# Four query tiles transposed through DRAM and VectorE, and a routing table built from sign steps, in a fused attention and expert kernel

## The chip, the core and the metric

The kernel runs on one core of a Trainium2 chip. A core has a matrix engine (TensorE, PE in the profile; its weight loads are PEld), a vector engine (VectorE, DVE), an activation engine (ScalarE, ACT), a general engine (GpSimd, POOL) and an engine that issues transfers (SyncE, SP). Each works through its own list of instructions in the order in which the program issues them and waits on semaphores for the others. On-chip memory is SBUF (128 partitions); TensorE writes to PSUM, from which VectorE and ScalarE read. DRAM is reached by transfers (DMA), which SP and POOL issue here. The metric is the device time of one execution in microseconds (us).

## The reference

Two branches are added to the input x (2048 tokens of 512 values): linear attention over the normalized input, and a mixture of 8 experts of which each token uses its 2 best.

```python
xn = layernorm(x)
# A: 32 heads of 16
q, k, v = split(xn @ wqkv)
phi = lambda t: where(t > 0, t + 1, exp(t)) + 1e-6
kv = einsum("bhsd,bhse->bhde", phi(k), v);  z = phi(k).sum(tokens)
o = einsum("bhqd,bhde->bhqe", phi(q), kv) / (einsum("bhqd,bhd->bhq", phi(q), z) + 1e-6)
A = o.reshape(B, S, D) @ wo
# B: top 2 of 8 experts, softmax over the two logits
logits = xn @ w_gate;  gates = softmax(top 2 of logits)
B = sum over experts e of gate[e] * (silu(xn @ w1[e]) @ w2[e])
out = x + A + B
```

## The kernel before

The tokens are cut into 16 tiles of 128 (`NT`). Products keep near-full precision by splitting each operand into a high and a low part and adding three products, high by high, high by low, low by high (`PASSES`); a projection of a tile over 512 values is therefore 12 matmuls (4 slices of 128 by 3 passes). The high part is a copy on ScalarE (`split_hi`, line 141), the low part a subtraction on VectorE (`split_lo`, line 144).

The program runs in stages, each handed to the engines in program order (the manual schedule), so the order of the calls in the code is the order on every engine:

1. Load, layer norm and the projection of k for all tiles, and the sums that give the matrix M (kv times wo, kept as high and low parts in `M_v`).
2. The q tiles. This is the stage that the change touches. Tile numbers t run from 0; the code's tiles 6 to 9 are the seventh to the tenth.
3. The experts in 8 rounds, one weight pair after another; tokens are gathered from DRAM, the results are scattered into the output.
4. In the last expert round and behind it, the output projections of the last five q tiles (`ND = 5`, `NO = 11`).

In stage 2 a loop runs over t = 4 to 13. A q tile goes through these calls:

- `q_proj(t)`: 12 matmuls (line 1376), then three activations on ScalarE (lines 1385 to 1387) that leave exp(min(q, 0)).
- `q_phi`, `q_mult` (together `q_feat`): VectorE adds max(q, 0) (line 1393), POOL multiplies by z (line 1397).
- `q_den(t - 1)` and `q_norm(t - 1)`, an iteration later: VectorE sums each head and takes the reciprocal (lines 1410 to 1415), POOL multiplies (line 1416).
- `q_transp(t - 2)`: four transposes on TensorE (line 1422) into PSUM, whose high and low parts go to `pqT`.
- `o_proj(t - 3)`: 12 matmuls with M (line 1437); each group of three reads the high part twice and the low part in its third. `o_out(t - 4)`, an iteration later, adds the result to x on VectorE (line 1478) and stores it (line 1480).

Tiles 11 to 15 take another way: after `q_norm` they are stored to DRAM (`pz_out`), read back late in the last expert round in four pieces that set 32-row blocks side by side (`pz_in`, line 1447), transposed on VectorE in 32 x 32 blocks (`q_turn`, line 1454), and split by `q_hi` and `q_lo`.

Into the same loop other work is woven. The routing's steps (`routing`, a generator; `side` hands out pieces until their costs reach `PERIOD = 2.6`) end in iteration 6 with each token's lane and block. `table(q)` for q = 0 to 3 in iterations 7 to 10 builds two one-hot arrays of 4 tiles each on VectorE, `ohl` over the 128 lanes (line 645) and `mvb` over the 66 blocks, times the token number (lines 647 and 650). `table_mm(q)` multiplies them on TensorE in 8 small matmuls (line 660), an iteration later (the list `late`, run as `due`); the last one runs at the end of iteration 10. `table_end` in iteration 11 (lines 666 to 673) turns the sums into the row numbers `gidx` and `sidx`. From iteration 11 on, `gather1` fetches the first expert's tokens on POOL (line 1047), `x_block` transposes them on TensorE (line 1093), and `plain_w` splits the first weights (ScalarE and VectorE, lines 141 and 144) that `fetch_w` has loaded since iteration 8.

SBUF tiles come from pools: `ta` (11 buffers of 520 words a partition), `um` and `tb` (20 of 1152 words), `sm` (18 of 1024 words), `stage` (3, for weights). A new tile waits until a buffer of its pool is free.

Of the kernel before, what the change touches and what calls it, by code (L numbers as in the profile page):

```python
# [20 lines left out]
P = 128  # L21
# [25 lines left out]
NO = NT - ND  # L47
NE = 12
# [37 lines left out]
def linear_attn_plus_moe(  # L86
# [25 lines left out]
    xs_d = tc.dram_tile((E * RB * P, D), F32, name="xs_d")  # L112
    gate_d = tc.dram_tile((E, BLK, P), F32, name="gate_d")
# [112 lines left out]
    def constants_b():  # L226
# [13 lines left out]
        iota(i_lane, [[1, P]])  # L240
        iota(i_blk, [[1, NB]])
# [202 lines left out]
    lane_f = rt.tile([P, NT, 2], F16, name="lane_f")  # L444
# [11 lines left out]
    def routing():  # L456
# [177 lines left out]
        V.tensor_copy(blk_f, la_i)  # L634
        yield 3.0

    tabp = {}

    def table(q):
        ts = slice(4 * q, 4 * q + 4)  # L640
        ohl = ta(f"ohl{q}", 8 * P, F16).rearrange("p (a b) -> p a b", a=8)
        mvb = ta(f"mvb{q}", 8 * NB, F16).rearrange("p (a b) -> p a b", a=8)
        la = lane_f[:, ts, :].rearrange("p t k -> p (t k)").unsqueeze(2)
        bl = blk_f[:, ts, :].rearrange("p t k -> p (t k)").unsqueeze(2)
        V.tensor_tensor(ohl, i_lane.unsqueeze(1).broadcast_to([P, 8, P]),
                        la.broadcast_to([P, 8, P]), op=ALU.is_equal)
        V.tensor_tensor(mvb, i_blk.unsqueeze(1).broadcast_to([P, 8, NB]),
                        bl.broadcast_to([P, 8, NB]), op=ALU.is_equal)
        m4 = mvb.rearrange("p (t k) b -> p t (k b)", k=2)
        V.tensor_tensor(m4, m4, i_tok[:, ts].unsqueeze(2).broadcast_to([P, 4, 2 * NB]), op=ALU.mult)  # L650
        tabm[q] = (ohl, mvb)

    tabm = {}

# [7 lines left out]

    def table_end():
        tab = wp.tile([P, 2, NB], F32, tag="tab", name="tab", bufs=1)
# [11 lines left out]
    def side_jobs():  # L676
        yield from routing()
        for q in range(4):
            table(q)
            late.append(lambda q=q: table_mm(q))  # L680
            yield 9.0
        table_end()
# [685 lines left out]
    pq, pz, pqT = {}, {}, {}  # L1368
# [43 lines left out]
    def q_norm(t):  # L1412
        den = dens.pop(t)
        V.tensor_scalar(den, den, 1e-6, None, op0=ALU.add)
        V.reciprocal(den, den)
        G.tensor_tensor(heads(pz[t]), heads(pq[t]),
                        den.unsqueeze(2).broadcast_to([P, H, DH]), op=ALU.mult)
# [21 lines left out]

    def pz_out(t):  # L1440
        Q.dma_start(pz_d[(t - NO) * P:(t - NO + 1) * P, :], pz.pop(t))

    def pz_in(t):
        pz[t] = ta(f"pzr{t}")
        rows = pz_d[(t - NO) * P:(t - NO + 1) * P, :].rearrange("(c j) (a f) -> a j c f", j=BLK, f=P)
        for a in range(4):
            Q.dma_start(pz[t][a * BLK:(a + 1) * BLK].rearrange("j (c f) -> j c f", f=P), rows[a])

    def q_turn(t):
        src = pz.pop(t).rearrange("p (c k i) -> p c k i", i=BLK, k=KC)  # L1450
        pz[t] = ta(f"pzt{t}")
# [4 lines left out]
    def q_hi(t):  # L1456
        pqT[t] = tb(f"pqT{t}").rearrange("p (h c) -> p h c", h=2)
        split_hi(pqT[t][:, 0], pz[t])
# [71 lines left out]

    for t in range(OLAG + 1, NT - 2):
        if t < NO + OLAG:
            o_out(t - OLAG - 1)
        due, late[:] = late[:], []
# [6 lines left out]
        q_den(t - 1)  # L1541
        if 8 <= t < 11:
            fetch_w()
        q_proj(t)
        for f in due:
            f()
        if t in (11, 12):
            gather1(0, 2 * t - 22)
        if t == 12:
            x_block(0, 0)  # L1550
# [3 lines left out]
        if t > NO:  # L1554
            pz_out(t - 1)
# [3 lines left out]
        if t < NO + 2:  # L1559
            load_x(t - 2)  # L1560
            q_transp(t - 2)
# [4 lines left out]
        while 3 in tabm:  # L1566
            late.pop(0)()
        if t in (11, 12):
            gather1(0, 2 * t - 21)
# [210 lines left out]
```

## Time and profile before

| | us |
|---|---|
| median of 3 runs (lowest, highest) | 826.55 (826.29, 827.29) |
| profiled execution | 826.48 |
| its span, from the first to the last instruction | 824.8 |
| TensorE busy | 820.3 (99%) |
| VectorE busy | 679.6 (82%) |
| ScalarE busy | 541.2 (66%) |
| POOL busy | 249.7 (30%) |

Rows of the order in time have the start and the duration in us, the engine, the line of the kernel, the instruction, its tiles as output<-input, shapes and a count of merged instructions; in brackets stands how long the engine was idle before it and what ended the wait. Rows of groups have the busy time, the mean in ns of one, and the idle time before them. Matmuls are pipelined: one of 512 columns lasts 0.39 us, but the next starts before it ends, so the distance of their starts is what one costs. A queue name with a q (SPq) marks the issue of a transfer, not its landing.

### The profile page before, as it was taken

How to read it: one execution, taken by the hardware profiler on the slowest of the kernel's cores; microseconds unless marked ns; L12 is line 12 of the kernel's file. 1: busy time of each engine (PE TensorE's matmuls, PEld its weight loads, DVE VectorE, ACT ScalarE, POOL GpSimd, SP SyncE). 2: the span in 40 equal slices, each digit the busy share in tenths (PEclk: the TensorE clock that was granted, in tenths of full speed). 3: DMA queues.
4: the chain of work that ended last, by engine and by line, in shares of the span. 5: the costliest groups of instructions: out<-in, count | busy, mean ns of one | idle time of the engine just before them, and what ended most of it. 6: DMA issues, size and time to landing. Idle time of an engine off the chain costs nothing. (4 is left out here: it accounts for less than half of the span.)

```text
span 824.8 us, 15897 instructions
## 1 busy us (share of the span) xinstructions
PE 820.3 (99%) x5361; PEld 752.1 (91%) x5361; DVE 679.6 (82%) x1470; ACT 541.2 (66%) x1162; POOL 249.7 (30%) x335
## 2 busy tenths in 40 slices
PE   9999999999999999999999999999999999999998
PEld 8999888889999999999999999999999888888886
DVE  7788889999878887878888788789888987887851
ACT  5575364358666768766876777677768766776650
POOL 5543224375310136121803250443127030012002
PEclk9999999999999999999999999999999999999999
DMA  5752136354764565566557464756576573249507
GB/s 168 252 199 87 52 135 202 128 183 166 234 200 135 152 197 108 145 166 184 131 136 187 151 143 136 206 130 161 155 190 130 161 188 113 84 132 232 154 1 178
DMA packets 106874, 127.69 MB, mean 155 GB/s; under 512 B 15198, under 2 KB 69854, under 8 KB 106758
## 3 DMA queue, kind: packets, MB, share of 16 engines
q1 hardware_dynamic: 92902, 106.43, 42.7%
q0 software_dynamic: 12880, 18.66, 11.8%
q10 hardware_dynamic: 1008, 1.57, 0.5%
q8 instruction: 43, 0.70, 0.3%
q14 instruction: 41, 0.34, 0.1%
HBM read 93.95 MB, written 31.09 MB: 152 GB/s over the span
## 5 line engine op out<-in xcount | busy, mean ns | idle before, releaser
L1174 POOL DMA_INDIRECT out_dram<-yo,sidx x22 | 35.1, 1595 | 282.6 <-DVE yo L1169 260.4
L1174 POOL DMA_INDIRECT out_dram<-yu,L x47 | 78.0, 1659 | 85.9 <-ACT yu L1267 59.0
L144 DVE TENSOR_TENSOR h<-hs,h 128x576 fp32r<-128x576 f32 (+7 forms) x112 | 77.7, 694 | 5.7 <-ACT h L141 5.4
L141 ACT ACTIVATE h<-hs 128x576 fp32r<-128x576 f32 (+7 forms) x112 | 72.3, 646 | 3.2
L1324 ACT ACTIVATE hs<-px 128x276 f32<-128x276 f32 (+7 forms) x54 | 21.1, 390 | 58.7 <-PE px L1316 58.6
L1339 ACT ACTIVATE hs<-hs 128x276 f32<-128x276 f32 (+7 forms) x54 | 23.0, 426 | 46.5 <-DVE hs L1338 46.5
L1338 DVE TENSOR_TENSOR hs<-pz,hs 128x276 f32<-128x276 f32 (+7 forms) x54 | 23.3, 431 | 34.6 <-PE pz L1316 34.0
L1343 DVE TENSOR_TENSOR hs<-px,hs 128x276 f32<-128x276 f32 (+7 forms) x54 | 23.3, 432 | 33.7 <-PE px L1316 33.7
L1047 POOL DMA_INDIRECT xg<-xn_d,gidx x37 | 40.8, 1104 | 28.2 <-DMA xq<-xs_d 7.2
L437 PE MATMUL gacc<-pkhl,xnhl 128*128 128x512 f32 x192 | 47.9, 397 | 0.0
L437 PEld LDWEIGHTS gacc<-pkhl,xnhl 128*128 128x128 f32 x192 | 34.8, 188 | 6.8
L1173 POOL MEMSET spacer<- 1x1 f32 x69 | 38.4, 557 | 6.8 <-DVE ws_3l L144 6.8
L1349 DVE TENSOR_TENSOR hs<-py,hs 128x276 f32<-128x276 f32 (+7 forms) x54 | 23.0, 426 | 13.7 <-PE py L1316 13.4
L1344 ACT ACTIVATE hs<-hs 128x276 f32<-128x276 f32 (+7 forms) x54 | 22.8, 422 | 17.0 <-DVE hs L1343 15.8
L411 POOL TENSOR_TENSOR zz<-zz,pk 128x512 f32<-128x512 f32 x14 | 18.2, 1300 | 48.3 <-DVE L L404 48.3
L1385 ACT ACTIVATE e_q<-qp 128x512 f32<-128x512 f32 x16 | 9.6, 598 | 35.4 <-PE qp L1376 31.7
L1198 PE MATMUL y<-w_1h,h 128*128 128x512 f32 (+2 forms) x88 | 32.0, 394 | 0.0
L1198 PE MATMUL y<-w_5h,h 128*128 128x512 f32 (+2 forms) x88 | 32.0, 394 | 0.0
L1198 PE MATMUL y<-w_2h,h 128*128 128x512 f32 (+2 forms) x88 | 32.0, 393 | 0.0
L1198 PE MATMUL y<-w_3h,h 128*128 128x512 f32 (+2 forms) x88 | 32.0, 393 | 0.0
L1198 PE MATMUL y<-w_0h,h 128*128 128x512 f32 (+2 forms) x88 | 32.0, 393 | 0.0
L1198 PE MATMUL y<-w_4h,h 128*128 128x512 f32 (+2 forms) x88 | 31.7, 393 | 0.0
(563 smaller groups left out, 3152.8 us busy)
## 6 DMA issues: line engine op xcount, KB each, us to landing
wst<-in_B_w_dram SPq DMA_DIRECT2D x196, 128.0 KB
wst<-in_B_w_dram SPq DMA_DIRECT2D x37, 512.0 KB
zz<-in_B_w_dram SPq DMA_DIRECT2D x26, 512.0 KB
xs_d<-xg SPq DMA_DIRECT2D x117, 64.0 KB
xq<-xs_d SPq DMA_DIRECT2D x28, 256.0 KB
x<-in_A_x_dram SPq DMA_DIRECT2D x27, 256.0 KB
xn_d<-xn SPq DMA_DIRECT2D x16, 256.0 KB
xnT<-xn SPq DMA_DIRECT2D x11, 256.0 KB
```

What stands on the lines that cost most here:

```text
L141: A.activation(hi, src, AF.Copy)
L144: V.tensor_tensor(lo, src, raw(hi), op=ALU.subtract)
L437: T.matmul(gacc[d], xnhl[:, a, d * P:(d + 1) * P], pkhl[:, b, :], start=(t == 0 and i == 0), stop=(t == NT - 1 and i == 2))
L1047: G.indirect_dma_start(out=raw(t), out_offset=None, in_=xn_d, in_offset=IOA(ap=gidx[:, b:b + 1], axis=0))
L1173: G.memset(spacer, 0.0)
L1174: st = G.indirect_dma_start(out=rows, out_offset=IOA(ap=idx, axis=0), in_=src, in_offset=None, compute_op=ALU.add).ins
L1198: T.matmul(ya[r, d][:m], h[a][:, d * P:d * P + m], w[b][:, n % 2, :], start=(first and i == 0), stop=(last and i == 2))
L1338: V.tensor_tensor(c12, pz_, c12, op=ALU.add)
L1339: A.activation(c12, c12, AF.Silu)
L1343: V.tensor_tensor(c22, px, c22, op=ALU.add)
L1344: A.activation(c22, c22, AF.Silu)
L1349: V.tensor_tensor(c11, pz_, c11, op=ALU.add)
```

## The change

- Tiles 6 to 9 (`TURNED`) no longer pass through the four transposes on TensorE. `q_norm` writes them in an order of columns that suits the 32 x 32 blocks; in the same iteration they are stored to DRAM (`pz_out`) and read back in four pieces (`pz_in`); an iteration later VectorE turns them (`q_turn`) and ScalarE takes the high part (`q_hi`); at the start of the iteration after that VectorE takes the low part (`q_lo`), behind `o_out`. `o_proj` keeps its place, three iterations behind the projection.
- The lane array is no longer a one-hot from VectorE. ScalarE writes eight rows of sign(lane of the token - i - 0.5) for each table group (`table_lanes`), four behind the exponentials of `q_proj`, four later in the iteration, in iterations 6 to 9. The table's sums are then differences short of a step: after the last table group they are split (`table_split`, start of iteration 11) and multiplied by a two-diagonal matrix (`table_diff`, two matmuls behind `q_proj(11)`), and `table_end` follows, ahead of `q_den(10)`. Five instructions on POOL build the matrix (`table_steps`, iteration 8).
- `fetch_w` of iterations 8 to 10 is issued behind the read-back instead of ahead of the projection. `x_block(0, 0)` moves from in front of the attention's transposes to behind `o_proj(9)` in iteration 12.
- The lane arrays, the read-back and the step matrix use the `um` pool; `pqT` of the turned tiles stays in the `sm` pool.

```diff
@@ -45,6 +45,7 @@
 PASSES = ((0, 0), (0, 1), (1, 0))
 ND = 5
 NO = NT - ND
+TURNED = range(6, NO - 1)
 NE = 12
 NP = NF // 2
 NPLAIN = 2
@@ -110,6 +111,7 @@
     M_d = tc.dram_tile((2, 2, P, SW), F32, name="M_d")
     pz_d = tc.dram_tile((ND * P, D), F32, name="pz_d")
     xs_d = tc.dram_tile((E * RB * P, D), F32, name="xs_d")
+    pq_d = tc.dram_tile((len(TURNED) * P, D), F32, name="pq_d")
     gate_d = tc.dram_tile((E, BLK, P), F32, name="gate_d")
     sx_d = tc.dram_tile((P, BLK), F32, name="sx_d")
 
@@ -238,6 +240,7 @@
         G.affine_select(out=bmask, in_=bmask, pattern=[[DH, 8], [0, DH]],
                         compare_op=ALU.is_ge, fill=0.0, base=DH - 1, channel_multiplier=-1)
         iota(i_lane, [[1, P]])
+        G.tensor_scalar(i_lane, i_lane, 0.5, None, op0=ALU.add)
         iota(i_blk, [[1, NB]])
         iota(i_ov, [[1, NOV]])
         iota(i_e8, [[0, NT], [1, E]], base=-E)
@@ -441,7 +444,7 @@
 
 
     rt = cst
-    lane_f = rt.tile([P, NT, 2], F16, name="lane_f")
+    lane_f = rt.tile([P, NT, 2], F32, name="lane_f")
     blk_f = rt.tile([P, NT, 2], F16, name="blk_f")
     ohr = rt.tile([P, E, E], F32, name="ohr")
     gate = rt.tile([P, OV0], F32, name="gate")
@@ -632,25 +635,43 @@
         V.tensor_copy(lane_f, la_i)
         V.tensor_scalar(la_i, sl_i, 7, None, op0=ALU.arith_shift_right)
         V.tensor_copy(blk_f, la_i)
+        lanes.append(0)
         yield 3.0
 
     tabp = {}
+
+    lanes = []
+
+    def table_lanes(h):
+        if not lanes or lanes[0] == 4:
+            return
+        q = lanes[0]
+        if h == 0:
+            tabm[q] = raw(um(f"ohl{q}"))[:, :4 * P].bitcast(F16).rearrange("p (a b) -> p a b", a=8)
+        la = lane_f[:, 4 * q:4 * q + 4, :].rearrange("p t k -> p (t k)")
+        for i in range(4 * h, 4 * h + 4):
+            A.activation(tabm[q][:, i, :], i_lane, AF.Sign, bias=la[:, i:i + 1], scale=-1.0)
+        lanes[0] += h
 
     def table(q):
         ts = slice(4 * q, 4 * q + 4)
-        ohl = ta(f"ohl{q}", 8 * P, F16).rearrange("p (a b) -> p a b", a=8)
         mvb = ta(f"mvb{q}", 8 * NB, F16).rearrange("p (a b) -> p a b", a=8)
-        la = lane_f[:, ts, :].rearrange("p t k -> p (t k)").unsqueeze(2)
         bl = blk_f[:, ts, :].rearrange("p t k -> p (t k)").unsqueeze(2)
-        V.tensor_tensor(ohl, i_lane.unsqueeze(1).broadcast_to([P, 8, P]),
-                        la.broadcast_to([P, 8, P]), op=ALU.is_equal)
         V.tensor_tensor(mvb, i_blk.unsqueeze(1).broadcast_to([P, 8, NB]),
                         bl.broadcast_to([P, 8, NB]), op=ALU.is_equal)
         m4 = mvb.rearrange("p (t k) b -> p t (k b)", k=2)
         V.tensor_tensor(m4, m4, i_tok[:, ts].unsqueeze(2).broadcast_to([P, 4, 2 * NB]), op=ALU.mult)
-        tabm[q] = (ohl, mvb)
+        tabm[q] = (tabm[q], mvb)
 
     tabm = {}
+
+    def table_steps():
+        step, tabp[2] = ta("step", P), um("step_r")[:, :P]
+        G.memset(step, 0.0)
+        for base, v in ((0, -0.5), (-1, 0.5), (P - 1, -0.5)):
+            G.affine_select(out=step, in_=step, pattern=[[1, P]], compare_op=ALU.not_equal,
+                            fill=v, base=base, channel_multiplier=-1)
+        G.tensor_copy(tabp[2], step)
 
     def table_mm(q):
         if q == 0:
@@ -660,8 +681,18 @@
             T.matmul(tabp[0], ohl[:, i, :], mvb[:, i, :],
                      start=(q == 0 and i == 0), stop=(q == 3 and i == 7))
 
+    def table_split():
+        tab = wp.tile([P, 2, NB], F32, tag="tab", name="tab", bufs=1)
+        hl = um("tabhl")
+        tabp[1] = tab, hl[:, :NB], hl[:, NB:2 * NB]
+        split(*tabp[1][1:], tabp[0])
+
+    def table_diff():
+        for i in range(2):
+            T.matmul(tabp[0], tabp[2], tabp[1][1 + i], start=(i == 0), stop=(i == 1))
+
     def table_end():
-        tab = wp.tile([P, 2, NB], F32, tag="tab", name="tab", bufs=1)
+        tab = tabp[1][0]
         t1, em = tab[:, 0, :], tab[:, 1, :]
         V.tensor_copy(t1, tabp[0])
         V.tensor_scalar(gidx, t1, -1.0, 0.0, op0=ALU.add, op1=ALU.max)
@@ -677,9 +708,10 @@
         yield from routing()
         for q in range(4):
             table(q)
+            if q == 1:
+                table_steps()
             late.append(lambda q=q: table_mm(q))
             yield 9.0
-        table_end()
 
     marks = []
     side = side_jobs()
@@ -1365,7 +1397,7 @@
         Q.dma_start(out[S + i * P:S + (i + n) * P, :].rearrange("(a p) d -> p a d", p=P),
                     zt.unsqueeze(1).broadcast_to([P, n, D]))
 
-    pq, pz, pqT = {}, {}, {}
+    pq, pz, pzt, pqT = {}, {}, {}, {}
 
     eq = {}
 
@@ -1413,8 +1445,11 @@
         den = dens.pop(t)
         V.tensor_scalar(den, den, 1e-6, None, op0=ALU.add)
         V.reciprocal(den, den)
-        G.tensor_tensor(heads(pz[t]), heads(pq[t]),
-                        den.unsqueeze(2).broadcast_to([P, H, DH]), op=ALU.mult)
+        out, src, den = heads(pz[t]), heads(pq[t]), den.unsqueeze(2).broadcast_to([P, H, DH])
+        if t in TURNED:
+            out = pz[t].rearrange("p (a k h d) -> p k a h d", a=4, k=KC, d=DH)
+            src, den = (ap.rearrange("p (k a h) d -> p k a h d", a=4, k=KC) for ap in (src, den))
+        G.tensor_tensor(out, src, den, op=ALU.mult)
 
     def q_transp(t):
         p = psm("tr", f"pqp{t}")
@@ -1437,24 +1472,32 @@
                     T.matmul(op, pqT[t][:, a, kc * P:(kc + 1) * P], M_v[kc // 2][b][:, kc % 2, cols],
                              start=(kc == 0 and i == 0), stop=(kc == KC - 1 and i == 2))
 
+    def rows_d(t):
+        return pq_d[(t - TURNED[0]) * P:(t - TURNED[0] + 1) * P, :] if t in TURNED else \
+            pz_d[(t - NO) * P:(t - NO + 1) * P, :]
+
     def pz_out(t):
-        Q.dma_start(pz_d[(t - NO) * P:(t - NO + 1) * P, :], pz.pop(t))
+        Q.dma_start(rows_d(t), pz.pop(t))
 
     def pz_in(t):
-        pz[t] = ta(f"pzr{t}")
-        rows = pz_d[(t - NO) * P:(t - NO + 1) * P, :].rearrange("(c j) (a f) -> a j c f", j=BLK, f=P)
+        if t in TURNED:
+            both = raw(tb(f"pzr{t}"))
+            pz[t], pzt[t] = both[:, :D], both[:, D:]
+        else:
+            pz[t] = ta(f"pzr{t}")
+        rows = rows_d(t).rearrange("(c j) (a f) -> a j c f", j=BLK, f=P)
         for a in range(4):
             Q.dma_start(pz[t][a * BLK:(a + 1) * BLK].rearrange("j (c f) -> j c f", f=P), rows[a])
 
     def q_turn(t):
         src = pz.pop(t).rearrange("p (c k i) -> p c k i", i=BLK, k=KC)
-        pz[t] = ta(f"pzt{t}")
+        pz[t] = pzt.pop(t) if t in TURNED else ta(f"pzt{t}")
         dst = pz[t].rearrange("p (k c j) -> p c k j", k=KC, j=BLK)
         for q in range(2):
             V.transpose(dst[:, :, 2 * q:2 * q + 2, :], src[:, :, 2 * q:2 * q + 2, :])
 
     def q_hi(t):
-        pqT[t] = tb(f"pqT{t}").rearrange("p (h c) -> p h c", h=2)
+        pqT[t] = (sm if t in TURNED else tb)(f"pqT{t}").rearrange("p (h c) -> p h c", h=2)
         split_hi(pqT[t][:, 0], pz[t])
 
     def q_lo(t):
@@ -1528,9 +1571,16 @@
     q_transp(1)
     q_feat(3)
 
+    done = []
     for t in range(OLAG + 1, NT - 2):
+        diff = done == [table_mm]
+        if diff:
+            table_split()
+            done.append(table_split)
         if t < NO + OLAG:
             o_out(t - OLAG - 1)
+        if t - 3 in TURNED:
+            q_lo(t - 3)
         due, late[:] = late[:], []
         spent = 0.0
         while spent < PERIOD:
@@ -1538,33 +1588,48 @@
             if c is None:
                 break
             spent += c
-        q_den(t - 1)
-        if 8 <= t < 11:
-            fetch_w()
+        if not diff:
+            q_den(t - 1)
         q_proj(t)
+        table_lanes(0)
         for f in due:
             f()
+        if diff:
+            table_diff()
+            table_end()
+            q_den(t - 1)
         if t in (11, 12):
             gather1(0, 2 * t - 22)
-        if t == 12:
-            x_block(0, 0)
         if t == 13:
             gather1(0, 4)
         q_norm(t - 1)
-        if t > NO:
+        if t > NO or t - 1 in TURNED:
             pz_out(t - 1)
         q_feat(t)
         if t == 4:
             Q.dma_start(out[NO * P:S, :], x[NO * P:S, :])
         if t < NO + 2:
             load_x(t - 2)
-            q_transp(t - 2)
+            if t - 1 in TURNED:
+                pz_in(t - 1)
+            if t - 2 in TURNED:
+                q_turn(t - 2)
+                q_hi(t - 2)
+            else:
+                q_transp(t - 2)
+        table_lanes(1)
+        if 8 <= t < 11:
+            fetch_w()
         if t >= 11:
             plain_w()
         if t - OLAG < NO - 1:
             o_proj(t - OLAG)
-        while 3 in tabm:
+        while 3 in tabm and type(tabm[3]) is tuple:
             late.pop(0)()
+            if 3 not in tabm:
+                done.append(table_mm)
+        if t == 12:
+            x_block(0, 0)
         if t in (11, 12):
             gather1(0, 2 * t - 21)
 
```

## The prediction

> **What bounds the kernel now.** I read the page first, then the busy time by stretch, then the order of the instructions of each engine in the stage that the change touches.
>
> ```profile
> span 824.8 us, 15897 instructions
> ...
> PE 820.3 (99%) x5361; PEld 752.1 (91%) x5361; DVE 679.6 (82%) x1470; ACT 541.2 (66%) x1162; POOL 249.7 (30%) x335
> ```
>
> TensorE works 820.3 of 824.8 us, so the time falls only by work taken from TensorE, and rises by every wait put on it. The profiled execution took 826.48 us (1.68 around its span), 0.07 under the median of 826.55; the sum is made against 826.48. A change under 0.2% (1.65 us) can't be told from none here.
>
> ```profile
> 146.00:152.00 6.00, 6.00 (x30) 4.96 (x29) 5.90 (x10) 2.44 (x4) 2.21 (x3) 1.00 0.26 87
> ...
> 170.00:176.00 6.00, 6.00 (x30) 4.93 (x29) 5.65 (x14) 3.39 (x5) 4.87 (x5) 1.00 0.37 74
> ```
>
> By stretch (columns PE, PEld, DVE, ACT, POOL, clock, DMA share, GB/s): in the loop of the q tiles VectorE is as full as TensorE (5.90 of 6.00), ScalarE has 3.5 us to spare, the DMA engines three quarters. TensorE never waits, at full clock. The stage is balanced: each tile passes through all engines once, and whatever is late on VectorE comes to TensorE one or two tiles later.
>
> **1. What TensorE loses and gains.**
>
> ```profile
> 147.02 0.60 PE L1422 MATMUL pqp<-ident_r,pz 128*128 128x128 f32 x4
> ...
> 147.93 0.63 PE L1437 MATMUL op<-M0h,pqT 128*128 128x512 f32 x2
> ...
> 150.23 0.39 PE L1376 MATMUL qp<-wq0h,xnT 128*128 128x512 f32 x1
> ...
> 152.96 0.43 PE L660 MATMUL tabp<-mvb,ohl 128*128 128x66 f16 x8
> ...
> 154.16 0.62 PE L1437 MATMUL op<-M0h,pqT 128*128 128x512 f32 x2
> ...
> 159.83 0.48 PE L1437 MATMUL op<-M0h,pqT 128*128 128x512 f32 x1
> ...
> 168.86 0.43 PE L660 MATMUL tabp<-mvb,ohl 128*128 128x66 f16 x8
> ...
> 169.68 0.63 PE L1376 MATMUL qp<-wq0h,xnT 128*128 128x512 f32 x2
> ...
> 171.98 0.60 PE L1422 MATMUL pqp<-ident_r,pz 128*128 128x128 f32 x4
> ```
>
> A projection's 12 matmuls run from 150.23 to 152.96: 0.2275 each. From a transpose group (147.02) to the third matmul behind it (147.93) is 0.91; without the group it would be 2 x 0.2275, so a group costs 0.46. Behind a table group it is 1.20 with transposes (152.96 to 154.16) and 0.82 without (168.86 to 169.68): 0.38. Four groups go: those of tiles 6, 7, 8 (iterations 8 to 10, behind a table group) and 9 (iteration 11): 3 x 0.38 + 0.46 = 1.6. The two matmuls of table_diff come in: between a quarter of a table group (0.07) and a whole transpose group (0.46); I take half of the latter, 0.2. Net -1.4: 825.1, if nothing waits.
>
> **2. The new path of a q tile.** It was: q_norm (POOL), transposes (PE), hi (ACT), lo (DVE). It becomes: q_norm, pz_out (SP), landing, four pz_in (SP), landing, q_turn (DVE), hi, lo; q_turn two iterations behind the projection, lo three behind.
>
> ```profile
> L1454 DVE STREAM_TRANSPOSE pzt<-pzr x10: 401/419/440, 756.2 to 790.7; 128x256 f32<-128x256 f32 x10
> L141 ACT ACTIVATE pqT<-pzt x5: 615/624/639, 772.2 to 795.7; 128x512 fp32r<-128x512 f32 x5
> L144 DVE TENSOR_TENSOR pqT<-pzt,pqT x5: 682/686/692, 773.0 to 796.6; 128x512 fp32r<-128x512 f32 x5
> ```
> ```profile
> 0.83 0.86 SPq L155 DMA_DIRECT2D x<-in_A_x_dram  x2
> ```
> ```profile
> 3.49 0.69 DVE L273 BATCH_NORM_STATS2 bs<-x 128x6 f32<-128x512 f32 x1 [1.80 <-DMA x<-in_A_x_dram]
> ```
> ```profile
> 228.40 0.43 SPq L1237 DMA_DIRECT2D sx_d<-s_at  x1
> 234.81 1.75 SPq L1241 DMA_DIRECT2D s_in<-sx_d  x4
> ```
> ```profile
> 740.45 1.89 SPq L1447 DMA_DIRECT2D pzr<-pz_d  x4
> ```
>
> The last tiles already go this way: a turn is 2 x 0.42 = 0.84, hi 0.62, lo 0.69. The round trip is not in this stage. The one 256 KB transfer that something waits for at once, at the start, lands 2.66 after its issue (0.83 to 3.49); the four pz_in take 1.89 to issue. Lower end: 2.66 out, and back 2.66 from the first of the four issues: 5.3. Upper end: a store of the later stage, issued at 228.40 amid weight loads, whose reader could issue only at 234.81, 6.4; then 1.89 and 2.2 (2.66 less an issue of 0.43): 10.5. I take 2.66 + 1.89 + 1.9 = 6.5, nearest to the row at the start, as the DMA engines are a quarter to a half busy here; the weight loads behind pz_in are out of the way by the next pz_out.
>
> **3. Does it come in time?** Order of the engines from the code, durations from these rows, 0.1 a hand-over (estimate).
>
> ```profile
> 146.68 0.68 DVE L1478 TENSOR_TENSOR x<-op,x 128x512 f32<-128x512 f32 x1
> 147.28 1.88 DVE L645 TENSOR_TENSOR ohl<-i_lane,lane_f 128x1024 f16<-128x1024 f16 x1
> 149.08 0.70 DVE L647 TENSOR_TENSOR mvb<-i_blk,blk_f 128x528 f16<-128x528 f16 x1
> ...
> 150.44 0.68 DVE L1410 TENSOR_REDUCE den<-pz 128x32 f32<-128x512 f32 x1
> ...
> 151.64 0.63 DVE L1393 SCALAR_TENSOR_TENSOR pq<-qp,e_q 128x512 f32<-128x512 f32 x1
> ```
> ```profile
> 151.86 1.06 POOL L1416 TENSOR_TENSOR pz<-pq,den 128x512 f32<-128x512 f32 x1 [3.79 <-DVE den L1415]
> ```
>
> VectorE in iteration 7: o_out 0.60, lanes 1.80, mvb 1.36, then q_den(6); POOL's q_norm starts 1.42 behind q_den's start. The four lanes groups go (7.2 us of VectorE).
> - Tile 6: q_den at 150.44 - 1.80 = 148.64, q_norm 150.06 to 151.1, pz_out 151.2, + 6.5 = 157.7, turn to 158.65, hi to 159.4, lo to 160.2. o_proj(6) would start at 159.83 - 2 x 0.38 = 159.07, its third matmul (the first to read lo) 0.46 later. It waits 0.4 for hi and 0.3 for lo: **0.7**.
> - Tile 8 and table_diff: behind the turn of 6 VectorE still has lo(6) (160.2), mvb 1.36, then 1.42 to q_norm(8): 162.95, pz_out 164.1, + 6.5 = 170.6, turn(8) to 171.55. Behind it in VectorE's queue stands table_split, and on ScalarE hi(8) in front of its first half: 172.3, 172.6, then the low half: 172.9. table_diff needs it; TensorE is there at 171.98 - 3 x 0.38 + 0.7 = 171.5. It waits **1.4**.
> - o_proj(8): lo(8) is behind table_split and o_out(7): 172.9 + 0.6 + 0.7 = 174.2; its third matmul would be at 173.0 + 0.2 + 0.46 = 173.65. It waits **0.6**.
>
> ```profile
> 171.63 0.22 DVE L666 COPY tab<-tabp 128x66 f32<-128x66 f32 x1
> ...
> 172.88 0.68 DVE L1410 TENSOR_REDUCE den<-pz 128x32 f32<-128x512 f32 x1
> ...
> 175.67 2.43 DVE L144 TENSOR_TENSOR w_0l<-wst,w_0h 128x1024 fp32r<-128x1024 f32 x1
> ...
> 182.16 1.48 DVE L144 TENSOR_TENSOR w_1l<-wst,w_1h 128x1024 fp32r<-128x1024 f32 x1 [0.26 <-ACT w_1h L141]
> ```
> ```profile
> 174.58 1.05 ACT L141 ACTIVATE w_0h<-wst 128x1024 fp32r<-128x1024 f32 x1
> ```
>
> - o_proj(9), the largest: lo(9) stood ahead of the first weight split in iteration 11 and now stands behind it, in iteration 12. From 174.2: table_end 1.25 (171.63 to 172.88), q_den and q_norm 1.20, q_phi 0.55, turn(9) 0.84, hi(9) 0.72, the weights' high half 1.05 (ScalarE, behind hi(9)), their low half 1.6, o_out(8) 0.6, lo(9) 0.8: 182.8. TensorE: o_proj(8) from 173.2, + 0.6 + 24 x 0.2275 + 0.46 (transposes of tile 10) = 179.7, third matmul 180.2. It waits **2.6**, however fast the round trip is.
>
> The weights' low half took 2.43 beside POOL's q_mult and 1.48 in the iteration after. I take 1.48, as it now starts after q_mult(11) has ended; with 2.43 the sum is 1 us more. On this the Trainium skill, SBUF — State Buffer, section "Who interferes with whom", says that a VectorE instruction with two SBUF inputs contends with a GpSimd instruction that reads SBUF; by that rule lo(6), lo(8) and lo(9), which now read both inputs from SBUF, could be held by POOL too, and the sum would be up to 833 (three times the 0.95 between the rows). The two rows agree with it.
>
> Sum: -1.4 + 0.7 + 1.4 + 0.6 + 2.6 = +3.9: **830.3** (826.48 + 3.85 unrounded). Nothing behind this stage gives it back, since TensorE is full to the end.
>
> **4. What costs nothing.** Each at zero for the cover named.
>
> ```profile
> L1267 ACT ACTIVATE yu<-yu,gu 128x128 f32<-128x128 f32 x47 | 15.3, 389 | 1.3 <-DVE yu L1274 1.3
> ...
> L141 ACT ACT_TABLE_LOAD x1 | 1.3, 1283 | 0.8 <-PEq L1769 0.8
> L1296 ACT ACT_TABLE_LOAD x1 | 1.3, 1283 | 0.0
> ```
> ```profile
> masks.py:199 POOL TENSOR_SCALAR_AFFINE_SELECT idt<-idt 128x128 f32<-128x128 f32 x1 | 0.3, 292 | 0.1
> ```
>
> The Sign steps: like yu's (15.3 / 47 = 0.33), eight are 2.6 a tile; ScalarE goes from 2.44 to 5.0 of 5.7 in iterations 6 to 9. The second half stands behind hi, which waits for the turn, so the exponentials behind it can start 1 to 2 late; they have an iteration of slack. table_steps: five instructions of at most 0.3 on POOL, inside its wait of 3.79. On SP, pz_in waits for pz_out's landing with fetch_w and the next o_out store behind it: the weights are wanted from 174.58 on and are asked for from 160 on. q_norm's permuted write I keep at 1.06; were it twice that, each round trip would be 1 longer. x_block(0,0) moves back by a projection: no work more or less.
>
> **Rivals.**
> - *All in time (not slower)*: round trips of 5.3 and the work between table_diff and lo(9) 2.6 shorter than the rows say: 825.1. For it: VectorE loses 7.2 us of lanes. Against it: the order of iteration 12. It decides where lo(9) is ready at 180.2 minus the waits before. 0.20.
> - *The gathers take it back*: TensorE in time, but the first expert's rows not.
>
> ```profile
> 184.80 0.95 POOL L1047 DMA_INDIRECT xg<-xn_d,gidx  x1 [0.30 <-issue]
> ```
> ```profile
> DMA to landing us min/median/max: 5.2/5.2/5.2
> ```
> ```profile
> 190.34 0.80 PE L1093 MATMUL xep<-ident_r,xg 128*128 128x128 f32 x8
> ```
>
> The last gather lands at 190.0 and is read by the second half of the group at 190.34: 0.65 of slack. table_end now comes behind q_proj(11), so TensorE may gain 1.4 and the gathers only some 0.5: it waits about 0.3 to 1.2 and the time is 825.4 to 826.3. 0.10.
> - *Slow round trips*: 8.5 or more, as in the stage with weight loads. Each us counts twice (tiles 6 and 8): over 834.3, and 838.3 at 10.5. 0.12.
> - *Sign reloads the function table*: two loads of 1.28 in each of iterations 6 to 9 make ScalarE 5.0 + 2.6 = 7.6 of 5.7: 4 x 1.9 = 7.6, with the waits for lo(8) and lo(9) 826.48 - 1.4 + 7.6 + 3.2 = 836. The program has two loads in all, so Relu, Exp, Identity and Copy share one. The Trainium skill, ScalarE: Activation LUTs, section "Table sets: the hidden batching unit", has cheap functions in every set and doesn't name Sign among them. 0.03.
>
> **Numbers.** Forecast, a round trip of 5.3 to 8.5: 0.55, its own range 828.2 (the first two waits nearly gone, -1.4 + 0.1 + 0.5 + 2.6) to 834.3. Slower by over 0.2%: 0.55 + 0.12 + 0.03 = 0.70. The first rival's 825.1 is inside 0.2%; I give 0.07 of its 0.20 to faster and 0.13 to same, with the gathers 0.23. The range 825.0 to 834.5 leaves out the slow round trips, the table loads and the low edge of the first rival.
>
> **What would show it.** No transposes of q tiles between 153 and 172; TensorE idle before o_proj(6), table_diff, o_proj(8) and most before o_proj(9), each ended by VectorE's lo or split; VectorE idle before q_turn, ended by the read-back's DMA; SP from pz_out to the last pz_in about 4.5. Wrong if lo(9) runs before TensorE reaches o_proj(9), or if pz_out's landing takes under 1.5.

## The result, and the profile after

| | before | changed |
|---|---|---|
| median of the runs, us | 826.99 (6 runs, 826.29 to 827.33) | 837.43 (6 runs, 834.31 to 838.49) |
| profiled execution, us | 826.48 | 835.63 |
| span, mean granted clock | 824.8, 1.000 | 833.9, 0.998 |

The changed kernel is slower by 1.2% (ratio 1.012, interval 1.0102 to 1.0138). The direction was forecast, the size was not: 830.3 stands against 837.43, and the range ended at 834.5. The runs of the changed kernel lie 4 us apart, with mean clocks of 0.993 to 0.998; those before lie 1 us apart.

First the weight loads of TensorE (PEld) in order of time, only the rows with a wait; in brackets the idle time ahead of the instruction and what ended it.

```profile
159.28 0.30 PEld L1472 LDWEIGHTS op<-M0h,pqT 128*128 128x128 f32 x2 [0.20 <-DVE pqT L146]
...
165.54 0.19 PEld L1472 LDWEIGHTS op<-M0h,pqT 128*128 128x128 f32 x1 [0.83 <-ACT pqT L143]
...
166.27 0.30 PEld L1472 LDWEIGHTS op<-M0h,pqT 128*128 128x128 f32 x2 [0.43 <-DVE pqT L146]
...
174.41 0.30 PEld L692 LDWEIGHTS tabp<-tabhl,step_r 128*128 128x128 f32 x2 [2.87 <-issue]
...
175.55 0.30 PEld L1472 LDWEIGHTS op<-M0h,pqT 128*128 128x128 f32 x2 [0.61 <-DVE pqT L146]
...
182.59 0.19 PEld L1472 LDWEIGHTS op<-M0h,pqT 128*128 128x128 f32 x1 [1.54 <-ACT pqT L143]
...
186.00 0.30 PEld L1472 LDWEIGHTS op<-M0h,pqT 128*128 128x128 f32 x2 [3.11 <-DVE pqT L146]
```

In order these are `o_proj(6)`, twice `o_proj(7)`, `table_diff` ("issue", because the wait is for a split that VectorE ends at 174.3), `o_proj(8)`, twice `o_proj(9)`: 9.6 us together.

What is late lies on SP. Its queue of DMA issues (start, us, what):

```profile
151.59 0.33 SPq L1480 DMA_DIRECT2D pq_d<-pz  x1
...
153.66 1.76 SPq L1490 DMA_DIRECT2D pzr<-pq_d  x4
155.52 0.38 SPq L1523 DMA_DIRECT2D out_dram<-x  x1
156.60 0.34 SPq L1480 DMA_DIRECT2D pq_d<-pz  x1
...
160.57 1.75 SPq L1490 DMA_DIRECT2D pzr<-pq_d  x4
163.41 0.43 SPq L965 DMA_DIRECT2D wst<-in_B_w_dram  x1
163.94 0.45 SPq L1523 DMA_DIRECT2D out_dram<-x  x1
164.44 0.42 SPq L1480 DMA_DIRECT2D pq_d<-pz  x1
...
169.13 1.75 SPq L1490 DMA_DIRECT2D pzr<-pq_d  x4
171.09 0.41 SPq L965 DMA_DIRECT2D wst<-in_B_w_dram  x1
...
172.10 0.42 SPq L1480 DMA_DIRECT2D pq_d<-pz  x1
...
176.60 1.75 SPq L1490 DMA_DIRECT2D pzr<-pq_d  x4
```

And VectorE's turns, with the order behind the last one:

```profile
157.07 0.77 DVE L1497 STREAM_TRANSPOSE pzr<-pzr 128x256 f32<-128x256 f32 x2 [1.10 <-DMA pzr<-pq_d]
...
164.06 0.77 DVE L1497 STREAM_TRANSPOSE pzr<-pzr 128x256 f32<-128x256 f32 x2 [1.72 <-DMA pzr<-pq_d]
...
172.49 0.77 DVE L1497 STREAM_TRANSPOSE pzr<-pzr 128x256 f32<-128x256 f32 x2 [3.17 <-DMA pzr<-pq_d]
...
181.10 0.77 DVE L1497 STREAM_TRANSPOSE pzr<-pzr 128x256 f32<-128x256 f32 x2 [2.75 <-DMA pzr<-pq_d]
183.52 1.23 DVE L146 TENSOR_TENSOR w_0l<-wst,w_0h 128x1024 fp32r<-128x1024 f32 x1 [1.65 <-ACT w_0h L143]
184.66 0.68 DVE L1521 TENSOR_TENSOR x<-op,x 128x512 f32<-128x512 f32 x1
185.27 0.68 DVE L146 TENSOR_TENSOR pqT<-pzr,pqT 128x512 fp32r<-128x512 f32 x1
```

From `pz_out` to the turn (the round trip), tiles 6 to 9 take 5.5, 7.5, 8.05 and 9.0. The way back (first `pz_in` to turn) is 3.4, 3.5, 3.4, 4.5; the landing of `pz_out` (to the first `pz_in`) is 2.1, 4.0, 4.7, 4.5. Ahead of the `pz_out` of tiles 8 and 9 stands a weight load of 512 KB, issued 1.0 earlier. Why the way back of tile 9 is longer than the others isn't shown.

The `pz_out` of tiles 8 and 9 are also issued late. POOL's `q_norm` of these tiles:

```profile
161.94 1.06 POOL L1452 TENSOR_TENSOR pz<-pq,den 128x512 f32<-128x512 f32 x1 [4.11 <-DVE den L1447]
...
168.92 1.06 POOL L1452 TENSOR_TENSOR pz<-pq,den 128x512 f32<-128x512 f32 x1 [4.67 <-DVE den L1447]
```

They end at 163.00 and 169.98. SP is then still at the transfers that stand ahead (the weight load and the store, for tile 9 also the read-back of tile 8), and issues `pz_out` 1.4 and 2.1 later. From the end of `q_norm` to the turn it is 9.5 and 11.1.

Last, the busy time by stretch behind the wait of 3.11; the third number from the end is the granted clock.

```profile
186.00:188.00 2.00, 2.00 (x7) 1.63 (x8) 1.93 (x5) 0.82 (x1) 0.70 (x1) 0.77 0.68 169
188.00:190.00 2.00, 2.00 (x9) 1.51 (x8) 2.00 (x3) 0.00 (x0) 2.00 (x2) 0.50 0.95 354
190.00:192.00 2.00, 2.00 (x10) 1.67 (x10) 1.97 (x4) 0.66 (x2) 1.57 (x2) 0.87 0.89 251
```

TensorE gets half its clock for some 3.4 us: 2 x (0.23 + 0.50 + 0.13) = 1.7 us lost. With the waits of the weight loads the whole is 826.48 - 1.4 (as forecast) + 9.6 + 1.7 = 836.4. The matmuls (PE) end a little after the weight loads begin to wait, and are idle for 7.3 at the same places; with that figure it is 834.1. The measured 835.63 lies between the two.

### The profile page after: what moved, and what is told of

Read it like the earlier page. It is cut to its first block, busy times and chain, and to the rows that moved or that the text cites. A ratio compares the mean times of both kernels' runs of the same rounds, so it can differ in the third digit from the quotient of the medians.

```text
span 833.9 us, 15951 instructions
## 1 busy us (share of the span) xinstructions
PE 821.9 (99%) x5347; PEld 751.4 (90%) x5347; DVE 676.5 (81%) x1475; ACT 551.3 (66%) x1195; POOL 252.5 (30%) x341
## 5 line engine op out<-in xcount | busy, mean ns | idle before, releaser
L1079 POOL DMA_INDIRECT xg<-xn_d,gidx x37 | 39.1, 1056 | 32.0 <-DMA xs_d<-xg 7.3
L1230 PE MATMUL y<-w_6h,h 128*128 128x512 f32 (+2 forms) x88 | 31.6, 394 | 0.0
```

Of the source, the lines that this page charges most:

```text
L1079: G.indirect_dma_start(out=raw(t), out_offset=None, in_=xn_d, in_offset=IOA(ap=gidx[:, b:b + 1], axis=0))
L1230: T.matmul(ya[r, d][:m], h[a][:, d * P:d * P + m], w[b][:, n % 2, :], start=(first and i == 0), stop=(last and i == 2))
```

## The experiments

### The weight loads away from the round trips

```diff
+        if 4 <= t < 7:
+            fetch_w()
         q_proj(t)
...
-        if 8 <= t < 11:
-            fetch_w()
```

> The three first weight loads go out in iterations 4 to 6, ahead of every round trip; all else as changed. In the changed kernel the round trips of tiles 6, 7, 8, 9 (issue of pz_out to start of q_turn) took 5.5, 7.5, 8.1, 9.0. Theory A (what stands just ahead of pz_out in SP's queue makes its landing late, the 256 KB store of o_out most): tile 7 had a store ahead and no weights, so tiles 8 and 9 fall to about 7.5 each; table_diff waits some 0.6 less, o_proj(9) 0.6 to 1 less at its first matmul; about 836 against 837.4. Theory B (the weight loads are the cause): tiles 8 and 9 fall to 5.5 as tile 6; table_diff's wait of 2.9 falls to 0.3 to 0.8 and o_proj(9)'s first wait of 1.5 goes: 833 to 834. If the trips don't change at all, neither holds.

831.03 (ratio to before 1.0043, 1.0029 to 1.0057): 6.4 us of the 10.4 are gone, more than either theory said (between the two profiled executions it is 4.6, 835.63 to 831.07). `q_norm(8)` and SP's queue around tile 8, with a 256 KB store ahead and no weights:

```profile
162.89 1.06 POOL L1452 TENSOR_TENSOR pz<-pq,den 128x512 f32<-128x512 f32 x1 [4.11 <-DMA pzr<-pq_d]
```
```profile
163.12 0.38 SPq L1523 DMA_DIRECT2D out_dram<-x  x1
163.98 0.34 SPq L1480 DMA_DIRECT2D pq_d<-pz  x1
...
166.04 1.74 SPq L1490 DMA_DIRECT2D pzr<-pq_d  x4
```

`pz_out` goes out 0.03 behind the end of `q_norm`. The landing is 2.06 instead of 4.69, the trips of tiles 8 and 9 are at most 5.9 and 5.8. Theory B holds for the trips; the time fell below its 833. The waits of `table_diff`, `o_proj(8)` and the first of `o_proj(9)` are gone. Of TensorE's waits this one is left beside tile 7's 0.51 and 0.43 and tile 6's 0.18:

```profile
181.36 0.30 PEld L1472 LDWEIGHTS op<-M0h,pqT 128*128 128x128 f32 x2 [2.60 <-DVE pqT L146]
```

That is the third matmul of `o_proj(9)`, and the clock falls behind it too (0.72, 0.50, 0.93 from 182 to 188: again 1.7).

### The same loads on another queue

In `fetch_w` the three first loads are issued with `A.dma_start` instead of `Q.dma_start`, in the same iterations.

> The three first weight loads stay at their places in iterations 8 to 10 but are issued on ScalarE's DMA queue instead of SP's; all else as changed. Theory A (a weight load delays the round trip because pz_out stands behind it in the same queue): the landings of pz_out of tiles 8 and 9 fall from 4.7 and 4.5 to 2.1 to 3, and most of what the early loads brought (6.4) comes: 831 to 833. Rival B (the 512 KB take the DMA engines' time, whatever the queue): the landings stay at 4 or more and the time at 835.5 to 837.5.

830.75 (1.0051, 1.0038 to 1.0064). The landings of tiles 8 and 9 fall to 2.7 and 2.1, as theory A says, and their `pz_out` again goes out 0.03 behind `q_norm`. But the run doesn't settle queue against engines: on ScalarE the loads no longer wait behind `pz_in`, and go out 4 to 5.5 us earlier (159.5, 166.2, 173.0; on SP 163.4, 171.1, 178.5). The one at 166.2 now runs beside tile 8's read-back, and that takes 5.7 instead of 3.4; the one at 173.0 runs beside tile 9's, which takes 4.95:

```profile
166.19 0.41 ACTq L961 DMA_DIRECT2D wst<-in_B_w_dram  x1
```
```profile
172.09 0.77 DVE L1516 STREAM_TRANSPOSE pzr<-pzr 128x256 f32<-128x256 f32 x2 [1.61 <-DMA pzr<-pq_d]
...
178.19 0.77 DVE L1516 STREAM_TRANSPOSE pzr<-pzr 128x256 f32<-128x256 f32 x2 [0.19 <-DMA pzr<-pq_d]
```

So the trip itself stays long (8.4 and 7.0): what runs beside a load is slow on the other queue too. Counted from the end of `q_norm`, tiles 8 and 9 reach the turn after 8.4 and 7.1, against 9.5 and 11.1 with the loads on SP and 5.9 and 5.9 with the loads early.

### lo(9) ahead of the weight split

```diff
-        if t - 3 in TURNED:
+        if t - 3 in TURNED and t < 12:
             q_lo(t - 3)
...
+        if t == 11:
+            q_lo(9)
         if t >= 11:
             plain_w()
```

> q_lo(9) stands right behind q_hi(9) in iteration 11, ahead of the first weight split. Theory (the order of VectorE's queue holds o_proj(9), as the prediction says): the wait of 3.1 before its third matmul falls to 0.6 to 0.9 (hi and then lo, 0.63 and 0.68), the one before its first (1.5, the round trip) stays; 2.3 less, and 1 to 2 more if the lower clock that follows goes with it: 833.5 to 835 against 837.4. Rival (the weights' low half is then late and holds the first expert's work): the 2.3 comes back as a wait of TensorE after 190, time within 1 of 837.4.

834.24, 3.2 less, as expected (1.0085, 1.0072 to 1.0099). The wait of 3.11 is 0.43:

```profile
184.21 0.30 PEld L1472 LDWEIGHTS op<-M0h,pqT 128*128 128x128 f32 x2 [0.43 <-DVE pqT L146]
```

Between the profiled executions it is only 1.5 less (835.63 to 834.11): the half clock now follows the wait of `table_diff` (2.97; 0.80, 0.50, 0.85 from 174 to 180), and the first expert's transposes wait 1.12, part of what the rival feared.

### The table's split ahead of q_turn(8)

`table_split()`, `q_turn(8)` and `q_hi(8)` are called in this order behind `table_mm(3)`, at the end of iteration 10.

> table_split stands ahead of q_turn(8) and hi(8) on VectorE and ScalarE (both sit idle there, 169 to 172.5). Theory A (the round trip of tile 8 is the cause, the order only shows it): table_diff no longer waits, but o_proj(8) then waits for hi(8) and lo(8) at nearly the same time, its first matmul at about 174.0 instead of 174.6, its third at 174.7 instead of 175.55; 0.8 less: about 836.6. Rival B (the order is the cause, as the prediction's second wait has it): the whole 2.9 goes: about 834.5 or less.

836.08 (1.0108, 1.0093 to 1.0124). That is nearer to theory A, but 1.4 less than the changed kernel isn't clear of its spread of 4 us. The profile shows where the wait went: `table_diff` waits no more, and `o_proj(8)` takes the wait over:

```profile
174.13 0.19 PEld L1472 LDWEIGHTS op<-M0h,pqT 128*128 128x128 f32 x1 [1.98 <-ACT pqT L143]
```

The order only showed the late trip. Behind `o_proj(9)`, with waits of 1.74 and 3.11, the clock was one half for 6.8 us here (0.53, 0.50, 0.50, 0.76 from 184 to 192).

### TensorE kept busy in its waits

```diff
+    def fill(t, n):
+        pre[t] = psm("acc", f"op{t}_0", D)
+        for _ in range(n):
+            T.matmul(pre[t], M_v[0][0][:, 0, :P], M_v[0][0][:, 0, :], start=True, stop=True)
...
         if diff:
+            fill(8, 13)
             table_diff()
...
+            if t == 12:
+                fill(9, 21)
             o_proj(t - OLAG)
```

> Twelve to thirteen idle matmuls of 128x512 (12 to 13 x 0.2275 = 2.9) are put ahead of table_diff and 21 (4.8) ahead of o_proj(9); they write a PSUM tile that the real group then starts afresh. TensorE works through its waits, which stay as they are. Theory A (the idle TensorE brings the lower granted clock, 0.77, 0.50 and 0.87 in the windows from 186 to 192): the clock stays at 1.00 there, the profiled execution loses 1.7 (835.6 to about 834), the median more (its runs have a mean clock of 0.993 to 0.998), and the runs lie within 1 us of each other. Rival B (the lower clock has another cause, such as the DMA load or the weight splits): the windows from 186 to 192 stay under 0.9 and the time stays at 836 to 838.

The clock does what theory A says: 0.999, 0.999, 1.000, 1.000 in four runs (0.993 to 0.998 without the filling), and behind `o_proj(9)`:

```profile
188.00:190.00 2.00, 2.00 (x10) 1.62 (x10) 1.93 (x6) 0.59 (x1) 0.95 (x1) 1.00 0.86 241
```

The time is 836.19 (834.47 to 836.62), only 1.2 less, which isn't clear of the changed kernel's spread, and its own spread isn't under 1. In the profiled run tile 9's trip took 10.4, and `o_proj(9)` waited another 1.25 behind the filling. That the idle TensorE brings the lower clock is shown; what it costs the median isn't measured by this run.

### Store and load behind the read-back

In the iterations of the trips, SP's order becomes pz_out, pz_in, store of `o_out`, `load_x`.

> In the iterations of the round trips the store of an older tile (256 KB) and the load of x (256 KB) stand behind pz_in in SP's queue instead of ahead of it and beside it; the weight loads stay where the change put them. Theory B (only the weight loads make the trips of tiles 8 and 9 late): these stay at 7.5 to 9, the waits of table_diff (2.9) and o_proj(9) stay, and the time is 836 to 837.5; tile 7's trip (7.5, no weights near it) may fall. Rival A (any 256 KB ahead of or beside pz_out does it): all trips come to 5.5 to 6, the time to 831 to 833, as with the weights moved away (831.03).

838.29 (1.0137, 1.0122 to 1.0152): no gain, so theory B again, but 0.8 worse than it allowed. VectorE's `o_out` then waits 1.2 and 1.4 for the later x, and lo stands behind it. Tile 7's `pz_out` now has the store and the load of the tile before right ahead and lands in 4.6. Why tile 7's landing is late with no weights near (3.6 to 5.0 wherever its `pz_out` comes 5 us behind tile 6's) stays open; it isn't the store alone, since tile 8 had one 0.86 ahead and landed in 2.06. In the run of the turned tiles alone, further down, tile 7's `pz_out` comes 6.1 behind tile 6's, when tile 6's read-back has ended, and lands in 2.04.

### All of these together

> Weight loads in iterations 4 to 6, store and load behind pz_in, table_split ahead of q_turn(8), q_lo(9) ahead of the first weight split. If the waits found so far are all that the change costs, TensorE has none left but some 0.4 where lo follows hi, the clock stays at 1.00, and the four transpose groups stay saved: 826.9 - 1.4 + 0.2 to 0.8, so 825.5 to 826.3, faster than before by 0.1%. Rival: something else of the change costs time (gathers, Sign steps, POOL against VectorE), and it stays over 827.

830.52 (1.0052, 1.0039 to 1.0066). The theory failed: `o_out` waited 1.9 and 1.1 for x in the same way, and `o_proj` 1.9 and 1.4 for lo; the first expert's transposes waited 1.45, which the rival had named with the gathers. Moving store and load was the mistake; it is left out below.

### The table part alone

`TURNED` is empty; everything else as changed.

> The table's part alone: no tile is turned (q tiles 7 to 10 are transposed by TensorE as before), the lanes are Sign steps on ScalarE, table_split and table_diff stay, the weight loads stay behind q_transp. Theory (all of the loss hangs on the round trips): table_diff adds 0.2 and waits at most some 0.5 for its split: 827 to 827.7. Rival (the table part has a cost of its own: the Sign steps on ScalarE, the longer mvb beside POOL, the later table_end): 828.5 or more.

826.81 against 826.87 (1.0002, 0.9993 to 1.0011), and TensorE waits nowhere in this stage, but for the 0.26 at each table group that the kernel before has too. Sign steps, split and difference cost nothing that can be measured: the loss comes with the turned tiles.

### The turned tiles alone

The table as before, on top of the next experiment's two edits.

> The turned tiles alone: the table is built as in the kernel before (one-hot lanes on VectorE, no Sign steps, no table_diff), with the weight loads in iterations 4 to 6 and q_lo(9) ahead of the first weight split. To be read beside the run with the same two edits and the new table (828.06). Theory (VectorE was full, 5.9 of 6.0, and the turn needs the room that the lanes leave): 1.88 - 0.08 more of VectorE in each of four iterations, the turns come 2 to 4 late, TensorE waits, 832 or more. Rival (VectorE's waits for the read-back leave room enough): within 1 of 828.

830.59 (1.0060, 1.0043 to 1.0078), 2.5 more than the same with the new table. The turns of tiles 7 and 8 start without a wait for their read-back (165.56 and 172.26), so VectorE is what is late there. The time lies between the two expectations: the room that the lanes leave on VectorE is needed, but less than I had said.

### Weights early and lo(9) early

> Weight loads in iterations 4 to 6 and q_lo(9) ahead of the first weight split, nothing else. With the weights away (831.03) TensorE still waited 0.2, 0.5, 0.4 at tiles 6 and 7 and 2.6 before the third matmul of o_proj(9), and ran at clocks of 0.72, 0.50 and 0.93 behind that (loss of 1.7). Theory (that wait is VectorE's order, the clock follows from the wait): both go: 831.0 - 2.6 - 1.7 + up to 0.4: 826.7 to 827.2, no difference from before. Rival (the clock falls for another reason): 828 to 829.

828.06 (1.0019, 1.0010 to 1.0028). The wait of 2.60 is gone and the clock is 1.00 in the profiled run, as the theory has it, yet about 1 us is missing: the time is the rival's, its reason is not. TensorE has a new wait, before the first expert's transposes:

```profile
190.95 0.40 PEld L1125 LDWEIGHTS xep<-ident_r,xg 128*128 128x128 f32 x4 [1.33 <-ACT xr L1128]
```

ScalarE is late there, because an exponential found its buffer held by `q_norm` on POOL:

```profile
188.12 0.60 ACT L1417 ACTIVATE e_q<-qp 128x512 f32<-128x512 f32 x1 [1.14 <-POOL pz L1452]
```

POOL had waited 1.1 for denominators behind the weight split, then took 2.27 for a `q_mult` (1.29 before), and its `q_norm(12)` stands behind two gathers:

```profile
181.30 1.06 POOL L1452 TENSOR_TENSOR pz<-pq,den 128x512 f32<-128x512 f32 x1 [1.12 <-DVE den L1447]
182.32 2.27 POOL L1429 TENSOR_TENSOR pz<-pq,zz 128x512 f32<-128x512 f32 x1
184.75 0.99 POOL L1079 DMA_INDIRECT xg<-xn_d,gidx  x1 [0.15 <-POOL pz L1429]
186.04 0.95 POOL L1079 DMA_INDIRECT xg<-xn_d,gidx  x1 [0.30 <-issue]
187.01 1.07 POOL L1452 TENSOR_TENSOR pz<-pq,den 128x512 f32<-128x512 f32 x1
```

### Three steps to a version without waits

Tile 7 transposed again, and the denominators of tile 11 ahead of the weight split:

```diff
-TURNED = range(6, NO - 1)
+TURNED = (6, 8, 9)
...
             q_lo(9)
+            q_den(t)
+            den_inv(t)
```

> A version meant to beat both: weight loads in iterations 4 to 6; tiles 6, 8 and 9 turned, tile 7 transposed by TensorE as before (its trip starts while tile 6's read-back still runs, and it alone still made TensorE wait, 0.6 and 0.43); q_lo(9) and the denominators of tile 11 ahead of the first weight split, so that POOL's q_norm(11) need not wait 1.1 for them. Theory (the wait of 1.3 and 0.3 of the first expert's transposes in the run with the weights away and q_lo(9) moved comes from POOL, whose q_norm held the exponentials): with that wait gone, 826.9 - 3 groups (0.38 + 0.38 + 0.46) + 0.2 for table_diff + 0.2 to 0.5 of waits = 825.9 to 826.3, 0.1% faster. Rival (POOL is full there whatever VectorE does, and takes back what TensorE gains): 826.7 to 827.2.

829.99 (1.0037, 1.0024 to 1.0050); profiled 828.56. All waits of `o_proj` are gone, but the expert's transposes wait 1.20 and 1.73: the last gather is issued at 184.86, as in the kernel before (184.80), whatever TensorE gained. POOL takes the gain back, as the rival says, and the time is over the rival's 827.2 too; the three runs above the profiled one had mean clocks of 0.997 and 0.998. Next the table is ended earlier:

```diff
+            q_proj(t, True, 0)
+            table_diff()
+            table_end()
+            q_lo(t - 3)
+            gather1(0, 0)
+            gather1(0, 1)
```

> As the version meant to beat both (weights in iterations 4 to 6, tile 7 transposed by TensorE, q_lo(9) and the denominators of tile 11 ahead of the first weight split; 829.99, its profiled execution 828.56 with waits of 1.20 and 1.73 before the first expert's transposes), but the table is ended earlier: table_split stands ahead of q_turn(8), table_diff in the middle of q_proj(11), table_end right behind it, and the first two gathers ahead of q_norm(10). POOL sat idle for 3.2 before the first gather, at 172.95. Theory (the gathers and POOL's chain behind them hold TensorE there): the first gather starts at 171 to 171.5, the last some 1.4 earlier, q_norm(12) too; the waits fall from 2.9 to 0 to 1.0 and the time to 826.0 to 827, with the clock at 1.00. Rival (the last gather's landing is late for the DMA engines' load, not for POOL): the second wait stays at 1 or more and the time over 827.5.

827.07 (1.0004, 0.9995 to 1.0013), just over what was expected; the first gather starts at 171.27 as the theory said, the last still at 185.12, which it did not. Of the waits 0.60 and 0.67 are left; POOL stood idle for 1.87 ahead of `q_norm(11)`. So the fourth gather goes into that gap:

> As the version with the table ended early (827.07; its profiled execution had waits of 0.60 and 0.67 before the first expert's transposes, and POOL idle for 1.87 before q_norm(11)), but the fourth gather stands ahead of q_norm(11) on POOL, in that idle time, and q_den(11) ahead of q_lo(9). Theory (what is left of the saving goes into POOL's chain, gathers and q_norm(12)): the last gather starts at about 183 instead of 185.1, q_norm(12) ends 1 to 2 earlier, both waits go, and the time is 825.6 to 826.2, 0.1% under before. Rival (the gathers' landing, not their start, or ScalarE's own order holds the transposes): a wait of 0.6 or more stays there, and the time stays within 0.5 of 827.

826.17 against 826.67 (ratio 0.9993, 0.9984 to 1.0003).

```profile
177.54 0.95 POOL L1079 DMA_INDIRECT xg<-xn_d,gidx  x1 [0.30 <-issue]
178.51 1.63 POOL L1457 TENSOR_TENSOR pz<-pq,den 128x512 f32<-128x512 f32 x1
...
183.82 0.99 POOL L1079 DMA_INDIRECT xg<-xn_d,gidx  x1 [1.90 <-PE qp L1410]
185.02 1.06 POOL L1457 TENSOR_TENSOR pz<-pq,den 128x512 f32<-128x512 f32 x1 [0.21 <-DVE den L1447]
```

The waits of TensorE (PEld) from 150 to 195, summed by line, are in this version

```profile
PEld L681 <- issue: 1.0, 4, 0.3
PEld op L1477 <- DVE pqT L146: 0.2, 1, 0.2
```

and the first row is there before as well (0.8 and 0.3, at `table_mm`). The theory on POOL's chain holds: the last gather starts 1.3 earlier, and both waits are gone. With three of the four tiles turned the change can be had without its losses, and is then even with the kernel before or 0.1% faster; the interval takes in 1.

## Why the prediction was wrong

| TensorE waits for | forecast | measured | with the weights early |
|---|---|---|---|
| `o_proj(6)` | 0.7 | 0.20 | 0.18 |
| `o_proj(7)` | none | 0.83 + 0.43 | 0.51 + 0.43 |
| `table_diff` | 1.4 | 2.87 | none |
| `o_proj(8)` | 0.6 | 0.61 | none |
| `o_proj(9)` | 2.6 | 1.54 + 3.11 | 2.60 |
| sum | 5.3 | 9.6 | 3.7 |

- **The step that failed** is the size of the round trip. I took 6.5 for every tile and wrote that "the weight loads behind pz_in are out of the way by the next pz_out". They are not: `pz_in` holds SP until `pz_out` has landed, and the load goes out behind it. The next tile's `pz_out` is then issued 1.4 to 2.1 behind `q_norm` (0.1 taken) and 1.0 behind the load, and its landing takes 2.6 longer (4.69 against 2.06). Undisturbed the trip is 5.5 to 5.9, under my 6.5; behind a load it is 8 to 9. The bounds of 5.3 and 10.5 held all four tiles. That the loads are the cause is shown by the run that moves them. Whether they act by their place in the queue or by sharing the DMA engines stays open. The Trainium skill, DMA: Bandwidth & Descriptors, section "Queues, rings and completion order", says that each DMA engine takes the descriptors of one ring in order. The landing behind the load agrees with it; that the read-back beside a load of the other queue was slow too (5.7) shows that order isn't all.
- **Luck**: I had `pz_out(8)` at 164.1, and it went out at 164.44. But `q_norm(8)` had ended at 163.00, 1.0 earlier than in my sum, and the queue took that away.
- I had followed SP's queue for what waits behind `pz_in`, and asked only whether the weights would be late. The question left out was what they stand in front of.
- **Tile 7** was not worked out at all. Its trip was 7.5 with no weights near, and cost 1.3.
- **"Slow round trips"**, at 0.12, was the rival that came nearest; its "over 834.3" was right. Its 8.5 or more held for tile 9 alone. That "each us counts twice (tiles 6 and 8)" was wrong: tile 6 came in time, tiles 7, 8 and 9 did not.
- **o_proj(9)**: the cause, lo(9) behind the weight split, was right: lo moved ahead takes the wait away. The 2.60 with the weights early is my 2.6 by luck. TensorE came 1.4 earlier than in my sum, and so did lo; from the turn to lo it took 4.1, not 4.8 (the low half of the weights 1.22, with 1.48 taken). And the turn still waited 0.75 for the read-back there, so "however fast the round trip is" isn't shown.
- **The clock** had no term in the sum: 1.7 us in the profiled run, whose mean clock (0.998) was the highest of the six.
- **The -1.4** was not contradicted. Without waits, and with three groups out, its terms give -1.0 (-0.38 - 0.38 - 0.46 + 0.2); measured is -0.5, with an interval of -1.3 to +0.2.
- **"The gathers take it back"** was hidden by the larger waits. When those were mended the expert's transposes waited 1.3 to 2.9, where 0.3 to 1.2 was forecast: POOL's chain of gathers and `q_norm` has no room for a TensorE that is 1 us earlier.
- **Costs at nothing**: four Sign steps take 1.26 to 1.28, and there are two table loads in all, as before. `table_steps` took 2.1 instead of at most 1.5, which nothing waits for. The rule on VectorE and GpSimd (the Trainium skill, SBUF — State Buffer, "Who interferes with whom") showed at another place than I weighed. In the changed kernel lo kept its 0.69, but two of the `mvb` compares took 1.36 instead of 0.70, where they now fall beside POOL's `q_mult`. In the run with tile 7 transposed again, lo(9) fell beside `q_mult` and took 1.49, so the weighed case does exist.

## What to carry to other kernels

A round trip through DRAM pays for what stands ahead of it in its queue, and for a load that runs beside it: before moving a bulk load behind a step, look for the next store on that queue that something waits for, and put the load a few iterations earlier. When one engine is full to the end, a gain on it counts only as far as the next chain (here POOL's gathers) can also be earlier. Look in the order of each engine for an operand split that stands behind a larger job it doesn't need; such a wait stayed (2.60) when the transfer had become fast.

## What the runs showed of the hardware that I had not expected

A wait of TensorE can cost more than its length. In three profiled runs, behind waits of 2.60, 2.97 (0.61 more close behind) and 3.11 us (1.54 close ahead) of the weight loads, or 2.17, 2.57 and 2.68 us of the matmuls, the granted clock was one half for about 3.4 us, a loss of 1.7 each time. In two more, behind 1.74 and 3.11 and behind 1.69 and 3.11, it was one half for 6.8 us, part of it before the wait had ended. Behind 1.98 it stayed at 1.00, and behind the 2.87 and 0.61 of the changed kernel's profiled run too, so it doesn't follow every such wait. With the waits filled the mean clock was 0.999 to 1.000. The Trainium skill, TensorE: Matmul & The Clock Gate, section "What's actually happening", has half rate after an idle window of about 3.4 us, in windows that run freely. The half clock and its length agree (6.8 is twice that window); that 2.60 us of waiting is enough, the runs show and the page's window alone would not give.

VectorE and POOL slowed each other in both directions. On POOL `q_mult` took 2.27 us instead of 1.29, and `q_norm(11)` 1.63 instead of 1.06, beside the weights' low halves; on VectorE an `mvb` compare took 1.36 instead of 0.70, and lo(9) 1.49 instead of 0.69, beside a `q_mult` of 1.3.
